# Low part of the first layer's weights summed on TensorE and written by ScalarE; the exponential of a block's weights one pair behind its subtraction

## The chip, the cores and the metric

The kernel runs on one core of one Trainium2 chip. Its time is the device time of one execution in microseconds; less is better. Three runs of the kernel before gave a median of 1271.37 us (1271.09 to 1273.05). One more execution was profiled; all durations below come from it.

## The reference

A dynamic convolution of 7 taps, whose weights are a softmax over the taps, is followed by two feed-forward layers, one with ELU and one with a hard swish. The weights w_in and w_out reach the kernel as 64-bit numbers, the activations in 32 bits.

```python
w = np.exp(wg - wg.max(-1)); w = w / (w.sum(-1) + 1e-9)      # (2, 4096, 8 heads, 7 taps)
x = einsum("bshk,bskhg->bshg", w, windows of x)               # 8192 tokens x 192
h = x @ w_in1                                                 # 192 x 2048
g = np.where(h > 0, h, np.exp(np.minimum(h, 0)) - 1)
x = g @ w_out1                                                # 2048 x 192
h = x @ w_in2
out = (h * np.clip(h + 3, 0, 6) / 6) @ w_out2
```

## The kernel before

**Blocks and pairs.** The 8192 tokens are cut into 16 blocks of 512. For each of the two layers (m) and each block (i) there are 8 *pairs* (q): a pair is two tiles of 128 of the 2048 hidden features. The list `cells` holds all 256 (m, i, q), and the main loop (L562) goes through them one by one; n is the number of the pair. In step n TensorE gets the first product of pair n (192 inputs to 2 x 128 features, into the PSUM banks `hset`) interleaved with the second product of pair n - 3 (2 x 128 features to 192 outputs, into the banks `acca` and `accb`). Both halves of TensorE's rows work side by side, so two matmuls of 64 rows and 512 columns run at once.

**High and low parts.** All products are made from a high and a low part (fp32r) of both factors: high by high, high by low, low by high. `round_g` (L440) writes the high part gh of the activations on ScalarE, `rest_g` (L444) the residual gl on VectorE.

**What follows a pair.** For both halves (k = 1, then 0): `act_a` (L428) makes relu and exp on ScalarE, `gate` (L448) ELU on VectorE. After the first half come `fold_b`, then `round_g` and `rest_g` of pair n - 1, then `fold_a`. `fold_b` (L301) is called three pairs after the last of a block: ScalarE copies accb into `fold` (L308). accb is one bank: the first second product of the next block waits for that copy. acca is two banks that alternate.

**Weights of layer one.** They are split in *units*: 8 of w_in (kind "i") and 8 of w_out ("o"), each 128 x 384. Group 0 is one unit, groups 1 to 7 two each, group 8 one. A unit passes `begin` (absolute value on ScalarE into a bank, `aux` or `acca[1]`), s0 to s2 (clamp, shift, sign: the high 32 bits of a double made into an fp32 number f), s3 (exponent on VectorE into `tr`, and ScalarE's copy of f as the high part), s4 (the double's low 32 bits scaled), s5 (f minus the high part) and s6 (plus the scaled low bits, written as the low part). s0 to s6 but for the copy are VectorE's. Groups 0 and 1 go ahead of the main loop, 2 and 3 in step 0, then one group per step up to step 5. Layer two's units go through the same steps, one per block of layer one, a few steps at a time (`Stream`, L488).

**The softmax and the convolution.** `attention` (L192) returns its work as a list: s0 (maximum and subtraction on VectorE, exponential on ScalarE), s1 (sum and reciprocal), s2 (product with it), then 14 operations on GpSimd that make the block's convolution. s0, s1, s2 of a later block are called in three successive steps, in the end of step n; from the third block on s0 falls on the step before that of `fold_b`. `prepare` (L274) transposes the block's result on TensorE, and ScalarE and VectorE (`xh`, `xl`) split it. For block 1 this is done in step 2, into the banks acca[0] and accb.

**Order.** The schedule is manual: every engine works in the order in which the program issues its instructions. DMAs stand on SP's queue; after the first steps they are kept in a list and issued at marks in TensorE's work (`transfers`).

Of the kernel before, what the change touches and what calls it, by code (L numbers as in the profile page):

```python
# [17 lines left out]
def kernel(  # L18
# [53 lines left out]
    accb, aux = psp.tile([P, 512], F32, name="accb"), psp.tile([P, 512], F32, name="aux")  # L72

    ident = cpool.tile([P, P], F32, name="ident")
    warm = cpool.tile([P, 1], F32, name="warm")


# [31 lines left out]
    class Unit:  # L109
# [19 lines left out]
        def begin(self):  # L129

            bank = acca[1] if self.m == 0 and self.kind == "o" else aux
            self.b = bank[:, 0:UN].bitcast(U32)
            nc.scalar.activation(self.b.bitcast(F32), self.hw.bitcast(F32), AF.Abs)

        def s0(self):
# [6 lines left out]

        def s2(self):
            nc.vector.scalar_tensor_tensor(
                self.b, self.hw, 0xC0000000, self.b, op0=ALU.bitwise_and, op1=ALU.bitwise_or)

        def s3(self):
            self.r = stage.tile([P, UN], U32, tag="tr", name="tr", bufs=2)
            nc.vector.tensor_scalar(self.r, self.b, 0xFF800000, None, op0=ALU.bitwise_and)
            hi, _, v = self.parts()  # L150
            nc.scalar.copy(hi, v(self.b.bitcast(F32)))  # L151

        def s4(self):
            f = self.r.bitcast(F32)
            nc.vector.scalar_tensor_tensor(f, self.lw, 2.0**-52, f, op0=ALU.mult, op1=ALU.mult)  # L155

        def s5(self):
            f, (hi, _, v) = self.b.bitcast(F32), self.parts()
# [33 lines left out]
    def attention(i):  # L192

        n = TM * H
        xt, w3 = blk.pop(i)
        shp = [P, n, K]
        tt = {}
        v = nc.vector
        hn = n // 2
        yt = xw.tile([P, 2 * N], F32, tag="y", name="y", bufs=YB)  # L200
        y, yd = yt[:, 0:XN].rearrange("p (t e) -> p t e", e=D), yt[:, XN:].rearrange("p (s c) -> p s c", s=2)
        ya[i] = y, yd
        tmp = xw.tile([P, TM, D], F32, tag="tmp", name="tmp")

        def s0():
            mx = tt["m"] = xw.tile([P, n, 1], F32, tag="mx", name="mx")
            v.tensor_reduce(mx, w3, axis=AX.X, op=ALU.max)
            v.tensor_tensor(w3, w3, mx.to_broadcast(shp), op=ALU.subtract)  # L208
            nc.scalar.activation(w3, w3, AF.Exp)

        def s1():
            s = tt["m"]
            v.tensor_reduce(s, w3, axis=AX.X, op=ALU.add)
            v.tensor_scalar_add(s, s, 1e-9)
            v.reciprocal(s, s)

        if i == 0:

            pw = hset[1][0][:, 0:hn * K].rearrange("p (a k) -> p a k", k=K)
            po = hset[0][0][:, 0:2 * D].rearrange("p (t e) -> p t e", e=D)  # L220
            hs = [(nc.vector, slice(0, 2), pw, po), (nc.gpsimd, slice(2, 4), w3[:, hn:, :], tmp[:, 0:2])]
        else:
            hs = [(nc.gpsimd, slice(0, TM), w3, tmp)]

        def s2():
            s = tt["m"]
            if i == 0:
                v.tensor_tensor(pw, w3[:, :hn, :], s[:, :hn, :].to_broadcast([P, hn, K]), op=ALU.mult)
                v.tensor_tensor(w3[:, hn:, :], w3[:, hn:, :], s[:, hn:, :].to_broadcast([P, hn, K]), op=ALU.mult)
            else:  # L230
                v.tensor_tensor(w3, w3, s.to_broadcast(shp), op=ALU.mult)

        def product(k):
            def s():
                for eng, t, w, o in hs:
                    nt = t.stop - t.start
                    xk = xt[:, t.start + k:t.stop + k, :].rearrange("p t (h g) -> p t h g", g=G)
                    wk = w[:, :, k:k + 1].to_broadcast([P, nt * H, G])
                    if k == K - 1:
                        o = y[:, t, :]  # L240
                    eng.tensor_tensor(  # L241
                        o.rearrange("p t (h g) -> p t h g", g=G), xk,
                        wk.rearrange("p (t h) g -> p t h g", h=H), op=ALU.mult)
            return s

        def add():
            for eng, t, _, o in hs:
                eng.tensor_tensor(y[:, t, :], y[:, t, :], o, op=ALU.add)

        def add_a():  # L250
            for eng, t, _, o in hs:
# [12 lines left out]

        steps = [s0, s1, s2, product(K - 1)]
        for k in range(K - 2, -1, -1):
            steps += [product(k)] + ([add] if k else [add_a, add_d])
        return steps
# [5 lines left out]
    def prepare(m, i):  # L274
# [2 lines left out]
        v = lambda t: t[:, 0].rearrange("p (h c) -> p h c", h=2)  # L277
        if m == 0:

            (y, yd), ps = ya.pop(i), hset[0] if i == 0 else (acca[0], accb) if i == 1 else (acca[i % 2], aux)  # L280
            for t in range(TM):
                for h, p in enumerate(half):
                    nc.tensor.transpose(ps[h][:, t * HP:(t + 1) * HP], y[p, t, 0:P], ident[p, p])  # L283
            for s in range(2):
                for h, p in enumerate(half):
                    nc.tensor.transpose(ps[h][:, HN + s * HP:HN + (s + 1) * HP], yd[p, s], ident[p, p])
            parts = [(ps[h][:, 0:XN // 2], (lambda h: lambda t: v(t)[:, h])(h)) for h in range(2)]
        else:
            parts = [(zin.pop(i)[:, 0:XN], lambda t: t[:, 0])]

        def split():
            for src, w in parts:
                nc.scalar.copy(w(X["h"]), src)
            for src, w in parts:
                nc.vector.tensor_tensor(w(X["l"]), src, w(X["h"]).bitcast(F32), op=ALU.subtract)
            for k in "hl":
                for a in range(2):
                    later(2, X[k][half[1 - a], 1].bitcast(F32), X[k][half[a], 0].bitcast(F32))
        return split

    def fold_b(m, i):  # L301
# [161 lines left out]
    first = {b: NQ * k for k, b in enumerate(order)}  # L463
    last = {b: NQ * k + NQ - 1 for k, b in enumerate(order)}
    prep = {b: max(0, first[b] - PREP) for b in order}
    prep[0, 1] = LAG - 1
    start2 = first[1, 0]
    ya, xts, rs, gg, blk, zs, zin, folds = {}, {}, {}, {}, {}, {}, {}, {}
    told = {}
# [43 lines left out]
    for n in range(2 * NQ):  # L513
        c = NQ * (n + 2) if n < NB - 2 else start2 + (NQ if n % 2 else 0)
        groups.append([("io"[n % 2], 1, n // 2)])
        wtasks.append([c - 3, c + (3 if n < NB - 2 else 2 if n % 2 else 6), 1])
    made = {}

    def want(n):
        if n < len(groups) and n not in made:  # L520
            made[n] = [Unit(*u) for u in groups[n]]

    def w_steps(n):
        def step(k, u):
            def s():
                if k < 0:
                    if u == 0:
                        want(n)
                        want(n + 1)
                    made[n][u].begin()  # L530
                else:
                    getattr(made[n][u], f"s{k}")()
            return s
        return [step(k, u) for k in range(-1, WS) for u in range(len(groups[n]))]

    wtasks = [
        [b, d, (WS + 1) * c, (lambda n: lambda: w_steps(n))(n)] for n, (b, d, c) in enumerate(wtasks) if n > 1]
    begin = {i: max(6, prep[0, i - 1]) for i in range(2, NB)}
    loads = {begin[i] - 5: i for i in begin}
    softmax = {}  # L540

    three = cpool.tile([P, 1], F32, name="three")
    with tc.manual_schedule():
        nc.vector.memset(three, 3.0)
        nc.scalar.activation(warm, three, AF.Exp)
        blk[0] = load_block(0, lambda: want(0))
        make_identity(nc, ident)
        blk[1] = load_block(1)

        todo = {"w": w_steps(0), "a": attention(0)}  # L550
        for k in "aaawwawawawawawaw":
            todo[k].pop(0)()
        for s in todo["a"] + todo["w"]:
            s()
        c1 = attention(1)
        for s in c1[:3]:
            s()
        prepare(0, 0)()
        for s in c1[3:] + w_steps(1):
            s()  # L560
        wst = Stream(wtasks)
        for n in range(len(cells) + LAG + 3):  # L562
            now = n
            jobs = []
            for m, i in order:
# [4 lines left out]
                if m and n == last[m, i] + LAG + 2 + (i < NB - 1):  # L570
                    jobs.append(give(i))
            matmuls(n)

            for k in (1, 0):
                if n < len(cells):
                    act_a(n, k)
                    gate(n, k)
                if not k:
                    continue
                for b in order:  # L580
                    if n == last[b] + LAG:
                        fold_b(*b)
                if 1 <= n <= len(cells):
                    round_g(n - 1)
                    rest_g(n - 1)
                for b in order:
                    if n == last[b] + LAG + 1:
                        fold_a(*b)
# [3 lines left out]
                f()  # L592
            for i in range(2, NB):

                k = n - (begin[i] - 3)
                if k == 0:
                    softmax[i] = attention(i)
                if 0 <= k < 3:
                    softmax[i].pop(0)()
                if k == 3:  # L600
                    for s in softmax.pop(i):
                        s()
            wst.run(n)
# [34 lines left out]
```

## Time and profile before

| | |
|---|---|
| median of 3 runs | 1271.37 us |
| profiled execution | 1270.2 us, its span 1268.4 us |
| TensorE busy | 1182.7 us, 93% |
| VectorE busy | 909.9 us, 72% |
| ScalarE busy | 849.8 us, 67% |
| GpSimd busy | 426.7 us, 34% |
| mean granted TensorE clock | 0.98 of full speed |

A busy share is a mean over stages with different limits: the first 100 us, in which weights are split, and the stretch behind them, in which TensorE seldom stands still, are read apart. Where an engine idles, the row says in brackets for how long and what ended it. On VectorE and ScalarE an instruction's listed duration is somewhat longer than the distance to the start of the next one; sums of a busy chain go from start to start.

### The profile page before, as it was taken

The page shows a single profiled execution, that of the slowest core. Times are in us where ns is not written, and L with a number is a line of the kernel's source. Part 1 is how long each engine was busy: PE and PEld are TensorE (multiplying, and loading weights), DVE is VectorE, ACT ScalarE, POOL GpSimd, SP SyncE. Part 2 cuts the span into 40 slices and gives each one's busy share as a digit, 9 for nine tenths or more (in the row PEclk, how much of TensorE's full clock was granted, in tenths as well). Part 3 has the DMA queues.
Part 4 walks back from the last instruction along what each step waited for, and adds up shares of the span by engine and source line. Part 5 has one row for each costly group of instructions (what it writes and reads, how often), then busy time and mean ns, then how long its engine had stood idle before and what let it go on. Part 6 is the DMA issues. An engine that isn't in the chain of part 4 may idle for free.

```text
span 1268.4 us, 25353 instructions
## 1 busy us (share of the span) xinstructions
PE 1182.7 (93%) x10112; PEld 1091.5 (86%) x10112; DVE 909.9 (72%) x1264; ACT 849.8 (67%) x1314; POOL 426.7 (34%) x234
## 2 busy tenths in 40 slices
PE   2379999999999999999999999999999999999998
PEld 1257898888888888888888899999999999999996
DVE  7998777877777877788777666666666666666663
ACT  2447778877787877787886556666665566666553
POOL 7408886666886666876300000000000000000000
PEclk9589999999999999999999999999999999999999
DMA  6421222112221212222111111111111111111110
GB/s 158 132 75 36 86 86 71 53 61 73 86 86 51 69 64 73 86 66 70 32 46 52 50 51 38 51 50 28 38 51 51 51 39 50 51 38 33 45 39 26
DMA packets 33686, 75.82 MB, mean 60 GB/s; under 512 B 4644, under 2 KB 17058, under 8 KB 33568
## 3 DMA queue, kind: packets, MB, share of 16 engines
q1 hardware_dynamic: 33568, 74.19, 20.4%
q8 instruction: 80, 1.31, 0.5%
q14 instruction: 38, 0.31, 0.1%
HBM read 36.43 MB, written 12.58 MB: 39 GB/s over the span
## 4 chain that ended last, share of the span: by engine, by line
PE 55%; DVE 1%; ACT 1%; issue 0%; DVEq 0%
PE h L415 25%; PE acca L415 17%; PE accb L415 12%; DVE gl L446 1%; DVE r L452 0%; PE acca L339 0%; PE aux L339 0%; ACT r L435 0%; ACT r L436 0%; ACT gh L442 0%; DVE tr L155 0%; DVE wt L208 0%; ACT fold L308 0%; PE acca L283 0%; DVE z L315 0%
## 5 line engine op out<-in xcount | busy, mean ns | idle before, releaser
L415 PE MATMUL h<-xh,wi_l 64*128 64x512 f32 x1536 | 566.5, 399 | 3.9 <-DVE wi_l L165 3.9
L415 PE MATMUL h<-xh,wi_h 64*128 64x512 f32 x1536 | 558.7, 398 | 7.4 <-ACT wi_h L151 2.8
L415 PE MATMUL acca<-gh,wo 64*128 64x512 f32 x2048 | 564.8, 395 | 0.3
L415 PE MATMUL h<-xl,wi_h 64*128 64x512 f32 x1536 | 555.6, 397 | 0.8 <-DMA xl<-xl 0.8
L446 DVE TENSOR_TENSOR gl<-r,gh 128x1024 fp32r<-128x1024 f32 x256 | 346.1, 1352 | 76.1 <-ACT gh L442 75.1
L415 PEld LDWEIGHTS acca<-gh,wo 64*128 64x128 f32 x2048 | 380.5, 186 | 18.5 <-SPq L419 2.4
L415 PE MATMUL accb<-gh,wo 64*128 64x512 f32 x1024 | 327.5, 399 | 45.0 <-ACT fold L308 22.7
L438 ACT ACTIVATE r<-h,three 128x512 f32<-128x512 f32 x256 | 176.5, 689 | 223.5 <-PE h L415 214.5
L415 PE MATMUL accb<-gl,wo 64*128 64x512 f32 x1024 | 323.1, 395 | 0.4 <-DVE gl L446 0.4
L415 PE MATMUL acca<-gl,wo 64*128 64x512 f32 x1024 | 321.3, 393 | 0.0
L415 PEld LDWEIGHTS h<-xh,wi_h 64*128 64x128 f32 x1536 | 277.7, 187 | 20.0 <-ACT wi_h L151 3.2
L415 PEld LDWEIGHTS h<-xh,wi_l 64*128 64x128 f32 x1536 | 278.2, 187 | 16.2 <-DVE wi_l L165 5.0
L455 DVE SCALAR_TENSOR_TENSOR r<-r,h 128x512 f32<-128x512 f32 x256 | 175.8, 687 | 161.6 <-ACT r L438 160.7
L415 PEld LDWEIGHTS h<-xl,wi_h 64*128 64x128 f32 x1536 | 277.8, 187 | 12.7 <-DMA xl<-xl 1.5
L442 ACT CAST gh<-r 128x1024 fp32r<-128x1024 f32 x256 | 266.2, 1040 | 3.7 <-DVE r L452 1.8
L452 DVE SCALAR_TENSOR_TENSOR r<-r,h 128x512 f32<-128x512 f32 x256 | 174.8, 683 | 93.4 <-ACT r L436 92.5
L415 PEld LDWEIGHTS accb<-gh,wo 64*128 64x128 f32 x1024 | 187.6, 187 | 58.0 <-ACT fold L308 28.5
L241 POOL TENSOR_TENSOR tmp<-xt,wt 128x768 f32<-128x768 f32 (+1 forms) x96 | 196.0, 2042 | 7.3 <-DMA xt<-in_x_dram 1.1
L415 PEld LDWEIGHTS accb<-gl,wo 64*128 64x128 f32 x1024 | 190.6, 186 | 8.0 <-DVE gl L446 0.8
L415 PEld LDWEIGHTS acca<-gl,wo 64*128 64x128 f32 x1024 | 190.2, 186 | 7.9
L435 ACT ACTIVATE r<-h 128x512 f32<-128x512 f32 x256 | 152.8, 597 | 54.4 <-PE acca L415 35.9
L436 ACT ACTIVATE r<-r 128x512 f32<-128x512 f32 x256 | 161.9, 633 | 8.3
(87 smaller groups left out, 704.4 us busy)
## 6 DMA issues: line engine op xcount, KB each, us to landing
xt<-in_x_dram SPq DMA_DIRECT2D x14, 960.0 KB, 4.8
xh<-xh SPq DMA_DIRECT2D x64, 192.0 KB, 2.7
xl<-xl SPq DMA_DIRECT2D x64, 192.0 KB, 2.9
raw<-in_moe_w_out_dram SPq DMA_DIRECT2D x16, 384.0 KB, 3.3
z<-z SPq DMA_DIRECT2D x16, 384.0 KB, 2.3
zin<-z SPq DMA_DIRECT2D x16, 384.0 KB, 3.0
out_dram<-ot SPq DMA_DIRECT2D x16, 384.0 KB, 3.9
raw<-in_moe_w_in_dram SPq DMA_DIRECT2D x16, 192.0 KB, 3.3
```

The lines of the kernel that those rows point to most:

```text
L241: eng.tensor_tensor(o.rearrange("p t (h g) -> p t h g", g=G), xk, wk.rearrange("p (t h) g -> p t h g", h=H), op=ALU.mult)
L415: mm = nc.tensor.matmul(o, w, r, start=st, stop=sp).ins
L435: nc.scalar.activation(r, h, AF.Relu, scale=-1.0)
L436: nc.scalar.activation(r, r, AF.Exp, scale=-1.0)
L438: nc.scalar.activation(r, h, AF.Relu, bias=three)
L442: nc.scalar.copy(gg[n][0], rs[n])
L446: nc.vector.tensor_tensor(gl, rs.pop(n), gh.bitcast(F32), op=ALU.subtract)
L452: nc.vector.scalar_tensor_tensor(r, r, -1.0, h, op0=ALU.add, op1=ALU.max)
L455: nc.vector.scalar_tensor_tensor(r, r, 6.0, h, op0=ALU.min, op1=ALU.mult)
```

## The change

**Weights of layer one.** s5 and s6 are gone for layer one. Instead f is written to a buffer in SBUF, s4 writes its result as fp32r (`rr`), and TensorE sums f times the identity, the high part times the negative identity and rr times the identity into the unit's bank (p5, after the matmuls of a step); ScalarE copies the sum out as the low part (p6, behind relu and exp of both halves). For groups 4 to 8 the absolute value is written into the SBUF buffer as well, and s0 to s3 work there. In the steps below 8 `round_g` and `rest_g` come after p6.

**Softmax.** The exponential is a step of its own, s0e, one pair behind the subtraction; the list starts two steps earlier and the load of its block three steps earlier. The convolution keeps its step.

**Also moved.** From step 8 on `round_g` and `rest_g` come ahead of `fold_b`. `prepare` of block 1 goes from step 2 to step 5 and uses hset[0] in place of acca[0] and accb.

```diff
+            if self.m == 0:
+                self.ps = bank[:, 0:UN]
+                self.f = fts[self.n][:, self.u * UN:(self.u + 1) * UN].bitcast(U32)
+                if self.n > 3:
+                    self.b = self.f
+            else:
+                self.f = self.b
             nc.scalar.activation(self.b.bitcast(F32), self.hw.bitcast(F32), AF.Abs)
...
+        def p5(self):
+
+            hi, _, v = self.parts()
+            nc.tensor.matmul(self.ps, ident, self.f.bitcast(F32), start=True, stop=False)
+            nc.tensor.matmul(v(self.ps), minus, hi, start=False, stop=False)
+            nc.tensor.matmul(self.ps, plus, self.rr, start=False, stop=True)
+
+        def p6(self):
+            _, los, v = self.parts()
+            for lo, c in los:
+                nc.scalar.copy(lo, v(self.ps)[..., c])
...
             v.tensor_tensor(w3, w3, mx.to_broadcast(shp), op=ALU.subtract)
+
+        def s0e():
             nc.scalar.activation(w3, w3, AF.Exp)
...
-            (y, yd), ps = ya.pop(i), hset[0] if i == 0 else (acca[0], accb) if i == 1 else (acca[i % 2], aux)
+            (y, yd), ps = ya.pop(i), hset[0] if i < 2 else (acca[i % 2], aux)
...
-    prep[0, 1] = LAG - 1
+    prep[0, 1] = 5
...
-    loads = {begin[i] - 5: i for i in begin}
+    loads = {max(0, begin[i] - 8): i for i in begin}
...
             matmuls(n)
+            if n < NQ:
+                for u in made[n + 1]:
+                    u.p5()
 
             for k in (1, 0):
                 if n < len(cells):
                     act_a(n, k)
                     gate(n, k)
+                if not k and n < NQ:
+                    for u in made[n + 1]:
+                        u.p6()
+                if k == (n >= NQ) and 1 <= n <= len(cells):
+                    round_g(n - 1)
+                    rest_g(n - 1)
                 if not k:
                     continue
                 for b in order:
                     if n == last[b] + LAG:
                         fold_b(*b)
-                if 1 <= n <= len(cells):
-                    round_g(n - 1)
-                    rest_g(n - 1)
...
-                k = n - (begin[i] - 3)
+                k = n - (begin[i] - 5)
```

Three places show what the edits do to the order. First ScalarE at a block boundary of layer one, before; L435 and L436 are relu and exp of a half, L209 the exponential of the softmax, L308 the fold, L442 gh.

```order
L442 CAST gh<-r 128x1024
L435 ACTIVATE r<-h_74 128x512
L436 ACTIVATE r<-r 128x512
L209 ACTIVATE wt<-wt 128x224
L435 ACTIVATE r<-h_73 128x512
L436 ACTIVATE r<-r 128x512
L308 COPY fold<-accb 128x512
L442 CAST gh<-r 128x1024
```

The same place with the change (L459, L460 are relu and exp, L332 is the fold, L466 gh):

```order
L459 ACTIVATE r<-h_74 128x512
L460 ACTIVATE r<-r 128x512
L459 ACTIVATE r<-h_73 128x512
L460 ACTIVATE r<-r 128x512
L466 CAST gh<-r 128x1024
L332 COPY fold<-accb 128x512
```

The exponential no longer stands between the relu and exp of the two pairs, and gh has moved from behind the fold to ahead of it.

Second, VectorE some two pairs earlier, with the change; L476 are gates, L470 is gl, L229 and L230 are the maximum and the subtraction, L157 is s3 of a unit of layer two.

```order
L476 SCALAR_TENSOR_TENSOR r<-r,h_75 128x512
L470 TENSOR_TENSOR gl<-r,gh 128x1024
L476 SCALAR_TENSOR_TENSOR r<-r,h_74 128x512
L229 TENSOR_REDUCE mx<-wt 128x32
L230 TENSOR_TENSOR wt<-wt,mx 128x224
L157 TENSOR_SCALAR tr<-aux 128x384
L476 SCALAR_TENSOR_TENSOR r<-r,h_73 128x512
L470 TENSOR_TENSOR gl<-r,gh 128x1024
```

Maximum and subtraction (L229, L230) have come to stand between the gate and s3; before, nothing stood there, and the two followed two pairs later:

```order
L452 SCALAR_TENSOR_TENSOR r<-r,h_74 128x512
L149 TENSOR_SCALAR tr<-aux 128x384
L452 SCALAR_TENSOR_TENSOR r<-r,h_73 128x512
L446 TENSOR_TENSOR gl<-r,gh 128x1024
L452 SCALAR_TENSOR_TENSOR r<-r,h_72 128x512
L155 SCALAR_TENSOR_TENSOR tr<-raw,tr 128x384
L452 SCALAR_TENSOR_TENSOR r<-r,h_75 128x512
L446 TENSOR_TENSOR gl<-r,gh 128x1024
L452 SCALAR_TENSOR_TENSOR r<-r,h_74 128x512
L207 TENSOR_REDUCE mx<-wt 128x32
L208 TENSOR_TENSOR wt<-wt,mx 128x224
```

Maximum and subtraction (L207, L208 there) stood directly behind the gate of the pair in which the fold comes; they have moved two pairs forward, ahead of an s3.

Third, ScalarE in one step of layer one's weights (step 2) with the change; L459 and L460 are relu and exp, L177 the low parts, L141 the absolute values of the next group, L159 its high parts.

```order
L459 ACTIVATE r<-h_73 128x512
L460 ACTIVATE r<-r 128x512
L459 ACTIVATE r<-h_72 128x512
L460 ACTIVATE r<-r 128x512
L177 CAST wi_l<-aux 128x384
L177 CAST wo_88<-acca_77 128x2x128
L177 CAST wo_88<-acca_77 128x2x64
L466 CAST gh<-r 128x1024
L233 ACTIVATE wt<-wt 128x224
L141 ACTIVATE f<-raw 128x384 x2
L159 CAST wi_h<-f 128x384
L159 CAST wo_88<-f 128x2x192
```

The low parts stand behind relu and exp of both halves and ahead of gh, and gh ahead of the next group's absolute values.

## Rows read from the trace of the kernel before

**Rows 1.** Busy by stretches: us, PE, PEld, DVE, ACT, POOL busy, TensorE's granted clock, DMA:

```profile
60.00:70.00 10.00, 7.77 (x44) 6.17 (x46) 9.27 (x20) 4.14 (x9) 0.00 (x0) 0.59 0.17 48
90.00:100.00 10.00, 7.33 (x37) 5.05 (x39) 9.83 (x17) 6.27 (x12) 6.63 (x4) 0.78 0.00 0
```

**Rows 2.** The waits of the whole span: who waited for whom, us, times, longest:

```profile
ACT wt L209 <- DVE wt L208: 45.8, 15, 7.6
...
PE accb L415 <- ACT fold L308: 22.7, 13, 2.4
```

**Rows 3.** Timeline of TensorE, a block boundary of layer two: start, us, work:

```profile
757.33 0.40 PE L415 MATMUL accb<-gh,wo 64*128 64x512 f32 x1
...
761.76 0.39 PE L415 MATMUL accb<-gh,wo 64*128 64x512 f32 x1
```

**Rows 4.** Timeline of TensorE, a block boundary of layer one:

```profile
225.10 0.40 PE L415 MATMUL accb<-gh,wo 64*128 64x512 f32 x1
...
231.41 0.49 PE L415 MATMUL accb<-gh,wo 64*128 64x512 f32 x1 [1.67 <-ACT fold L308]
```

**Rows 5.** Timeline of ScalarE, the same boundary:

```profile
218.89 0.48 ACT L151 CAST wi_h<-aux 128x384 fp32r<-128x384 f32 x1 [1.22 <-DVE tr L149]
...
229.35 0.39 ACT L209 ACTIVATE wt<-wt 128x224 f32<-128x224 f32 x1 [2.78 <-DVE wt L208]
...
230.79 0.57 ACT L308 COPY fold<-accb 128x512 f32<-128x512 f32 x1
```

**Rows 6.** Timeline of VectorE, the same boundary:

```profile
218.30 0.55 DVE L149 TENSOR_SCALAR tr<-aux 128x384 uint32<-128x384 uint32 x1
...
227.83 0.67 DVE L452 SCALAR_TENSOR_TENSOR r<-r,h 128x512 f32<-128x512 f32 x1
228.43 0.37 DVE L207 TENSOR_REDUCE mx<-wt 128x32 f32<-128x224 f32 x1
228.91 0.41 DVE L208 TENSOR_TENSOR wt<-wt,mx 128x224 f32<-128x224 f32 x1
```

**Rows 7.** Timeline of ScalarE, one step of the weights of layer one:

```profile
55.62 0.48 ACT L151 CAST wi_h<-aux 128x384 fp32r<-128x384 f32 x1 [4.77 <-DVE tr L149]
...
56.46 0.60 ACT L435 ACTIVATE r<-h 128x512 f32<-128x512 f32 x1
...
57.63 1.03 ACT L442 CAST gh<-r 128x1024 fp32r<-128x1024 f32 x1
...
58.57 0.59 ACT L435 ACTIVATE r<-h 128x512 f32<-128x512 f32 x1
```

**Rows 8.** Timeline of ScalarE, the boundary of layer two:

```profile
760.09 0.59 ACT L308 COPY fold<-accb 128x512 f32<-128x512 f32 x1 [0.17 <-PE accb L415]
```

**Rows 9.** The page, costliest groups: POOL's products of a block, mean ns behind the comma:

```profile
L241 POOL TENSOR_TENSOR tmp<-xt,wt 128x768 f32<-128x768 f32 (+1 forms) x96 | 196.0, 2042 | 7.3 <-DMA xt<-in_x_dram 1.1
```

**Rows 10.** Timeline of VectorE, the weights of layer one:

```profile
52.26 0.55 DVE L137 TENSOR_SCALAR aux<-aux 128x384 f32<-128x384 f32 x1
...
57.84 0.54 DVE L165 TENSOR_TENSOR wi_l<-aux,tr 128x384 fp32r<-128x384 f32 x1
58.31 0.60 DVE L165 TENSOR_TENSOR wo<-acca,tr 128x256 fp32r<-128x256 f32 x2
...
59.43 1.21 DVE L446 TENSOR_TENSOR gl<-r,gh 128x1024 fp32r<-128x1024 f32 x1
60.57 0.67 DVE L452 SCALAR_TENSOR_TENSOR r<-r,h 128x512 f32<-128x512 f32 x1
...
83.73 0.54 DVE L137 TENSOR_SCALAR aux<-aux 128x384 f32<-128x384 f32 x1
```

**Rows 11.** Timeline of TensorE, the same stage and the first boundary:

```profile
62.23 0.79 PE L415 MATMUL accb<-gh,wo 64*128 64x512 f32 x1 [14.03 <-DVE xl L295]
...
100.39 0.62 PE L415 MATMUL accb<-gh,wo 64*128 64x512 f32 x1
...
116.52 0.50 PE L415 MATMUL accb<-gh,wo 64*128 64x512 f32 x1 [1.05 <-ACT fold L308]
```

More of the change, by code (lines that the diff above doesn't have):

```diff
@@ L74 @@
     ident = cpool.tile([P, P], F32, name="ident")
+    plus, minus = (cpool.tile([P, P], F32R, name=n) for n in ("plus", "minus"))
     warm = cpool.tile([P, 1], F32, name="warm")
@@ L144, in s2 @@
             nc.vector.scalar_tensor_tensor(
-                self.b, self.hw, 0xC0000000, self.b, op0=ALU.bitwise_and, op1=ALU.bitwise_or)
+                self.f, self.hw, 0xC0000000, self.b, op0=ALU.bitwise_and, op1=ALU.bitwise_or)
         def s3(self):
             self.r = stage.tile([P, UN], U32, tag="tr", name="tr", bufs=2)
-            nc.vector.tensor_scalar(self.r, self.b, 0xFF800000, None, op0=ALU.bitwise_and)
+            nc.vector.tensor_scalar(self.r, self.f, 0xFF800000, None, op0=ALU.bitwise_and)
             hi, _, v = self.parts()
-            nc.scalar.copy(hi, v(self.b.bitcast(F32)))
+            nc.scalar.copy(hi, v(self.f.bitcast(F32)))
         def s4(self):
-            f = self.r.bitcast(F32)
-            nc.vector.scalar_tensor_tensor(f, self.lw, 2.0**-52, f, op0=ALU.mult, op1=ALU.mult)
+            f = o = self.r.bitcast(F32)
+            if self.m == 0:
+                o = self.rr = stage.tile([P, UN], F32R, tag="rr", name="rr", bufs=2)
+            nc.vector.scalar_tensor_tensor(o, self.lw, 2.0**-52, f, op0=ALU.mult, op1=ALU.mult)
+        def p5(self):
[7 more added lines that the diff above has]
+                nc.scalar.copy(lo, v(self.ps)[..., c])
         def s5(self):
@@ L262, in add_d @@
                     eng.tensor_tensor(yd.rearrange("p s (a e) -> p s a e", a=2), v(y), v(o), op=ALU.add)
-        steps = [s0, s1, s2, product(K - 1)]
+        steps = [s0, s0e, s1, s2, product(K - 1)]
         for k in range(K - 2, -1, -1):
@@ L297, in split @@
                 for a in range(2):
-                    later(2, X[k][half[1 - a], 1].bitcast(F32), X[k][half[a], 0].bitcast(F32))
+                    later(1 if (m, i) == (0, 1) else 2, X[k][half[1 - a], 1].bitcast(F32), X[k][half[a], 0].bitcast(F32))
         return split
@@ L516 @@
         wtasks.append([c - 3, c + (3 if n < NB - 2 else 2 if n % 2 else 6), 1])
-    made = {}
+    made, fts = {}, {}
     def want(n):
@@ L521, in want @@
             made[n] = [Unit(*u) for u in groups[n]]
+            for u, unit in enumerate(made[n]):
+                unit.n, unit.u = n, u
     def w_steps(n):
@@ L529, in s @@
                         want(n + 1)
+                        if groups[n][0][1] == 0:
+                            fts[n] = act.tile([P, XN], F32, tag="z", name="f", bufs=2)
                     made[n][u].begin()
@@ L533, in step @@
             return s
-        return [step(k, u) for k in range(-1, WS) for u in range(len(groups[n]))]
+        return [step(k, u) for k in range(-1, WS if groups[n][0][1] else 5) for u in range(len(groups[n]))]
     wtasks = [
-        [b, d, (WS + 1) * c, (lambda n: lambda: w_steps(n))(n)] for n, (b, d, c) in enumerate(wtasks) if n > 1]
+        [b, d, ((WS if groups[n][0][1] else 5) + 1) * c, (lambda n: lambda: w_steps(n))(n)] for n, (b, d, c) in enumerate(wtasks) if n > 1]
     begin = {i: max(6, prep[0, i - 1]) for i in range(2, NB)}
-    loads = {begin[i] - 5: i for i in begin}
+    loads = {max(0, begin[i] - 8): i for i in begin}
     softmax = {}
@@ L547 @@
         make_identity(nc, ident)
+        nc.scalar.copy(plus, ident)
+        nc.scalar.mul(minus, ident, -1.0)
         blk[1] = load_block(1)
         todo = {"w": w_steps(0), "a": attention(0)}
-        for k in "aaawwawawawawawaw":
+        for k in "aaaawwawawawaw":
             todo[k].pop(0)()
@@ L554 @@
             s()
+        made[0][0].p5()
+        made[0][0].p6()
         c1 = attention(1)
-        for s in c1[:3]:
+        for s in c1[:4]:
             s()
         prepare(0, 0)()
-        for s in c1[3:] + w_steps(1):
+        for s in c1[4:] + w_steps(1):
             s()
@@ L593 @@
             for i in range(2, NB):
-                k = n - (begin[i] - 3)
+                k = n - (begin[i] - 5)
                 if k == 0:
                     softmax[i] = attention(i)
-                if 0 <= k < 3:
+                if 0 <= k < 4:
                     softmax[i].pop(0)()
-                if k == 3:
+                if k == 5:
                     for s in softmax.pop(i):
```

## Prediction

> **What bounds the kernel now.** I read four views in this order: busy time by stretches, the waits, the timelines of the engines round one block boundary, and the timelines of the stage in which the first layer's weights are split.
>
> The stretches [rows 1] show two regimes. Between 60 and 100 us VectorE is busy 9.27 and 9.83 of 10 us, while TensorE has gaps and a granted clock of 0.59 and 0.78 of full speed: here VectorE's chain sets the pace. Behind that TensorE is the bound, and what counts is only the time in which it stands still.
>
> The waits [rows 2] name that time: TensorE waits 22.7 us, 13 times, for ScalarE's `fold` copy, which empties the bank accb at a boundary between two blocks. ScalarE itself waits 45.8 us, 15 times, for the softmax subtraction before its exponential.
>
> One boundary shows the link. A pair of TensorE takes 4.43 us (757.33 to 761.76 on the undisturbed boundary of layer two [rows 3]), so after 225.10 the next pair is due at 229.53; it starts at 231.41, 1.88 us late, and 1.67 of this are listed as idle [rows 4]. ScalarE sat 2.78 us before the exponential at 229.35, then did relu, exp and the fold at 230.79, which took 0.57 [rows 5]. VectorE was late with the subtraction (228.91), because the gate of the half before ran at 227.83 and the maximum at 228.43 [rows 6]. VectorE in turn was late through an earlier link: the copy of layer-two weights at 218.89 waited 1.22 us for VectorE's `tr` at 218.30, and relu, exp, gate and the next residual queue behind it.
>
> **The exponential a pair behind its subtraction.** The subtraction moves two pairs earlier, the exponential one, so ScalarE finds its operand ready: the 2.78 us go. What is late next? Two things are moved into this chain. First, maximum and subtraction (0.48 from start to start, then 0.41 long, some 0.8 together [rows 6]) now stand directly ahead of `tr`, so `tr`, the copy behind it, relu, exp and all gates up to the one at 227.83 come 0.8 us later: that gate runs 228.63 to 229.30. Second, `gh` of the pair before stands ahead of the fold now, and it needs this very gate. So gh starts at 229.35, takes 0.94 (57.63 to 58.57 [rows 7]), the fold runs 230.29 to 230.86, and TensorE starts at 230.91 instead of 231.41. Gain 0.5 us of 1.88 per boundary; 13 boundaries have an exponential in them, 6.5 us. The ends: the wait gone altogether gives 13 x 1.67 = 21.7 us; if VectorE's delay costs a full gh more, (0.94 - 0.5) x 13 = 5.7 us are lost. I take 6.5, since every link of it has a row.
>
> In layer two the fold also goes behind gh, at 16 boundaries. There ScalarE was early: the fold waited 0.17 us for accb [rows 8]. gh would start at 759.9, take 0.94, the fold end at 761.4; the bank is wanted at 761.76 [rows 3]. 0.35 us of cover are left, cost nothing; if gh came late by more than that, each further tenth costs 1.6 us over the 16.
>
> The loads of a block (two DMAs on SP's queue) go out three pairs earlier. Their buffers belong to the block two before, whose 14 GpSimd operations take 14 x 2.04 = 28.6 us [rows 9], 6.4 pairs, from a start 8 pairs ahead of the new load: 1.6 pairs of cover, some 7 us. Cost nothing.
>
> **The weights of layer one.** Each of 16 units loses the subtraction (0.47, from start to start, 57.84 to 58.31 [rows 10]) and the sum (0.47, or about 0.53 for the pair of the w_out units): 16 x 0.47 + 8 x 0.47 + 8 x 0.53 = 15.5 us of VectorE. If VectorE stayed the bound, the whole of it were won. It does not, because what replaces it is a ring through three engines. In one step: VectorE's first five operations on a pair of units, 5 x 0.47 = 2.35; ScalarE's two copies of the high part, 0.84; relu and exp of two halves, 2 x 1.17; the three new copies of the low part, 1.0 (the same columns as the 0.84, one instruction more); gh 0.94; VectorE's residual gl 1.14; hand-offs 0.2. Sum 8.8 us [rows 7, 10], and no link can overlap the next, since ScalarE works in program order: the low copies stand ahead of gh, gh ahead of gl, gl ahead of the next pair of units. TensorE's six new matmuls per step lie beside relu and exp: at the rate of the 512-column matmuls (0.23 at full, 0.43 at half clock) they are 1.1 to 1.9 us, under 2.34. The bank must be empty before the next Abs or the next sum: this adds waits only in the first steps.
>
> For true FP32 the Trainium skill (FP8 and Floating Point Precision, TensorE Precision Notes) says four passes; no matmul of this form is in the trace. By it, the identity product of each unit is four times as long, the six together about 1.9 at full and 3.8 at half clock, which at half clock would lengthen a ring by 1.5.
>
> The step of before is (83.73 - 52.26) / 3 = 10.5 us [rows 10]. Up to 52.26 seven units have been through, 6.8 us less work; against that come max and subtraction (0.8), waits for the emptied bank, and gh behind the low copies ahead of the first gl. I take a lead of 2 there (ends 0 and 6.8). Three rings and 1.3 us of softmax work make 27.7 instead of 31.5: lead 5.8.
>
> Now TensorE. The transposes of block 1 move from the third pair to the sixth and into the bank pair that the seventh pair (cell 6) wants, so cell 6 waits until VectorE's `xl` has read it, one ring and 0.9 us behind 83.73 - 5.8: 87.6. TensorE has then stood some 6 us. After the 14.03 us gap at 62.23 [rows 11] the clock of the next 10 us was 0.59 [rows 1], that is the lower level for more than half of it. I charge 2.8 us: cell 6 lasts until 94.8, relu, exp and low copies bring cell 7 to 97, cell 8 to 102.5. Before, cell 8 started at 100.39 [rows 11]. From there to the first boundary before took 16.13 us (116.52), now 3 x 4.43 and 0.6 of waiting, 13.9: 2.2 won back. So at 116.5 both kernels stand level. One price here is an upper bound: 0.47 is from operations whose operand lies in a PSUM bank, while Abs's result of groups 4 to 8 now lies in SBUF, and the trace has no such one-source operation of 384 columns. Its ends are 0.47 and a saving of almost all of it, 4 x 0.4 per ring in five rings, 8 us. I take 0.42, near the row: 1 us. The other end is 10 us lost, if TensorE ran at half clock in these cells and became the long link of the ring.
>
> Sum against the profiled execution, 1270.2 us (span 1268.4 and 1.8 around it): -6.5 - 1 = 1262.7. The median of the runs is 1271.4, 1.2 above it: 1264.
>
> **Rivals.** *The SBUF operations are twice as fast.* Streaming 384 columns at half the time saves 0.2 on each of the four on the ring, 0.8 in five rings, 4 us in place of 1: 1261. This is the Trainium skill's rule (VectorE: DVE Perf Modes, Mode 2x_2P: one source and the destination in SBUF); no operation in the trace shows it. Against it stands only that no row bears it out; for it that the bank was left for SBUF in five groups.
>
> *The fold's wait goes altogether.* If gh is ready early because the 0.8 us on VectorE vanish in its pauses, 21.7 - 1 in place of 6.5: 1264 - 15 = 1249. For it: in layer two, with no exponential, TensorE has no such wait. Against: the gate at 227.83 and the maximum behind it show no idle time ahead of them [rows 6]; there is no pause there to take the 0.8 up.
>
> *Nothing is won at the boundary*, since gh takes what the exponential gave back: 1270.
>
> *Slower.* The fold behind gh makes TensorE wait where it did not: in layer two, 16 times. It decides from 0.35 us of lateness on; one gh late by a whole 0.94 costs 0.6 x 16 = 9.5 us, less 7: 1274. For it: the cover is thin; against: ScalarE idles a microsecond ahead of each half there, so nothing makes gh late. The same time comes out if the setup runs at half clock (10 lost): 1274.
>
> **Numbers.** Forecast 0.36 (own range 1260 to 1268), twice as fast in SBUF 0.27, wait gone 0.12, nothing at the boundary 0.12, slower 0.13. What a measurement tells from no change is 0.2%, 2.5 us: faster than 1268.9 is 0.75 of it, within 0.13, slower 0.12. The range for eight in ten goes from half of the full gain, 1251, to just under the slower case, 1273.
>
> **What would show it.** Right: the 13 waits of accb for fold stand at about 1.2 us instead of 1.67, with gh directly ahead of the fold and a gate ahead of gh; no wait of the exponential for the subtraction; rings of 8 to 9 us in the setup, with VectorE idle before each gl; TensorE idle some 5 us ahead of cell 6. Wrong: boundaries without a wait; a setup in which VectorE is still busy throughout; new waits of accb in layer two; TensorE at the lower clock between 45 and 85 us.

## The result, and the profile after

The median went from 1271.69 us to 1255.23 us (4 runs each), a ratio of 0.9869 (95% interval 0.9852 to 0.9886): 16.5 us faster. The forecast was 1264, 7.4 us faster. The profiled execution took 1254.9 us, its span 1253.1, 15.3 less than before.

Where these microseconds went is read from one instruction that every block has, the fold on ScalarE. The distance from the start of one fold to the start of the next is the period of a block; the first fold closes the setup, the stage in which the weights of layer one are split.

| | before | after |
|---|---|---|
| first fold | 115.89 | 117.28 |
| period of a block, layer one (mean of the six distances between the folds of blocks 2 to 8) | 38.26 | 37.14 |
| first to 16th fold | 569.4 | 554.8 |
| period of a block, layer two | 35.84 | 35.84 |

So the setup lost 1.4 us and layer one won 14.6. The rest of the 15.3 is 1.5 at the change of layers, where two folds are 37.5 to 39.0 us apart even in kernels that are alike there, which is not explained here, and 0.6 at the end. There the last two folds are 33.1 to 33.2 us apart in the three kernels of this document that have gh ahead of the fold, and 33.8 in the others, so the 0.6 goes with that move.

The waits answer to [rows 2]: that of accb for the fold is 6.9 us in place of 22.7, and what is new is a wait of 5.0 us in the setup. ScalarE's exponential waits 4.8 us once, in place of 45.8 in 15 waits.

```profile
PE h L439 <- DVE xl L319: 7.6, 2, 5.0
...
PE accb L439 <- ACT fold L332: 6.9, 12, 0.6
...
ACT wt L233 <- DVE wt L230: 4.8, 1, 4.8
```

The boundary that answers to [rows 4 to 6], first TensorE, then ScalarE, then VectorE (start, us, work):

```profile
224.13 0.40 PE L439 MATMUL accb<-gh,wo 64*128 64x512 f32 x1
...
229.35 0.50 PE L439 MATMUL accb<-gh,wo 64*128 64x512 f32 x1 [0.57 <-ACT fold L332]
```

```profile
219.46 0.48 ACT L159 CAST wi_h<-aux 128x384 fp32r<-128x384 f32 x1 [2.77 <-DVE tr L157]
...
227.78 1.03 ACT L466 CAST gh<-r 128x1024 fp32r<-128x1024 f32 x1
228.72 0.58 ACT L332 COPY fold<-accb 128x512 f32<-128x512 f32 x1
```

```profile
215.06 2.24 DVE L470 TENSOR_TENSOR gl<-r,gh 128x1024 fp32r<-128x1024 f32 x1
...
218.30 0.65 DVE L230 TENSOR_TENSOR wt<-wt,mx 128x224 f32<-128x224 f32 x1
218.88 0.55 DVE L157 TENSOR_SCALAR tr<-aux 128x384 uint32<-128x384 uint32 x1
...
222.07 1.29 DVE L470 TENSOR_TENSOR gl<-r,gh 128x1024 fp32r<-128x1024 f32 x1 [0.25 <-ACT gh L466]
...
223.89 1.05 DVE L165 SCALAR_TENSOR_TENSOR tr<-raw,tr 128x384 f32<-128x384 uint32 x1
...
225.60 1.23 DVE L470 TENSOR_TENSOR gl<-r,gh 128x1024 fp32r<-128x1024 f32 x1
226.76 0.69 DVE L476 SCALAR_TENSOR_TENSOR r<-r,h 128x512 f32<-128x512 f32 x1
```

ScalarE waits 2.77 us for `tr`, and from 219.46 to the fold at 228.72 no row of it shows a pause. `gh` at 227.78, directly ahead of the fold, waits for nothing: its gate, 0.69 us from 226.76, ended 0.33 us earlier.

To set the two kernels side by side, count from the start of TensorE's pair ahead of the boundary: 225.10 before [rows 4], 224.13 after. From there the gate begins 2.63 us later; before, it was 2.73 [rows 6]. The forecast put it at 3.53 (228.63) and let it hold gh up.

Why was VectorE early? Its rows of before in the same stretch, to be set beside the two `gl` and the s4 above (1.29 at 222.07, 1.05 at 223.89, 1.23 at 225.60):

```profile
200.59 0.39 DVE L231 TENSOR_TENSOR wt<-wt,mx 128x224 f32<-128x224 f32 x1
...
221.51 1.78 DVE L446 TENSOR_TENSOR gl<-r,gh 128x1024 fp32r<-128x1024 f32 x1 [0.25 <-ACT gh L442]
...
223.81 1.61 DVE L155 SCALAR_TENSOR_TENSOR tr<-raw,tr 128x384 f32<-128x384 uint32 x1
...
225.94 1.97 DVE L446 TENSOR_TENSOR gl<-r,gh 128x1024 fp32r<-128x1024 f32 x1
```

Their 1.78, 1.61 and 1.97 us are not what these operations cost: alone, gl takes 1.23, and the second operation of s4 takes 0.55 (short convolution, below). Beside them GpSimd was at work on the convolution, until 229.91; after, it ends at 225.55. On the same count `tr` begins 1.55 us later than before (5.25 ahead of the pair in place of 6.80), not 0.8, as the gl ahead of it takes 2.24 beside GpSimd (215.06); the three operations, 1.79 us shorter together, give that back. First and last operation of GpSimd, before and after:

```profile
201.19 1.55 POOL L241 TENSOR_TENSOR y<-xt,wt 128x768 f32<-128x768 f32 x1 [9.53 <-PE accb L415]
...
229.02 0.89 POOL L262 TENSOR_TENSOR y<-y,tmp 128x256 f32<-128x256 f32 x1
```

```profile
197.71 1.64 POOL L265 TENSOR_TENSOR y<-xt,wt 128x768 f32<-128x768 f32 x1 [9.31 <-PE aux L310]
...
224.49 1.06 POOL L286 TENSOR_TENSOR y<-y,tmp 128x256 f32<-128x256 f32 x1
```

Before, the convolution began behind the product of the weights with the reciprocal (200.59 above). The change moves that product one pair forward with the list, so GpSimd now begins behind the transposes. Against the fold of its block it ends 3.2 us ahead in place of 0.9.

### The profile page after: what moved, and what is told of

It is laid out like the page before. It is cut to its first block, busy times and chain, and to the rows that moved or that the text cites. A ratio compares the mean times of both kernels' runs of the same rounds, so it can differ in the third digit from the quotient of the medians.

```text
span 1253.1 us, 25450 instructions
## 1 busy us (share of the span) xinstructions
PE 1200.7 (96%) x10176; PEld 1093.3 (87%) x10176; DVE 938.6 (75%) x1224; ACT 852.9 (68%) x1340; POOL 414.4 (33%) x234
## 4 chain that ended last, share of the span: by engine, by line
PE 68%; ACT 15%; DVE 12%; issue 3%; DMA 1%; SPq 0%; DVEq 0%; ACTq 0%
PE h L439 31%; PE acca L439 21%; PE accb L439 14%; DVE gl L470 5%; ACT gh L466 4%; ACT r L459 4%; ACT r L460 4%; DVE r L476 2%; DMA xl<-xl 1%; DVE tr L157 1%; DVE wt L230 1%; DVE aux L148 1%; DMA xt<-in_x_dram 1%; ACT fold L332 1%; ACT aux L141 0%
## 5 line engine op out<-in xcount | busy, mean ns | idle before, releaser
L470 DVE TENSOR_TENSOR gl<-r,gh 128x1024 fp32r<-128x1024 f32 x256 | 377.3, 1474 | 56.7 <-ACT gh L466 55.3
L439 PEld LDWEIGHTS h<-xh,wi_l 64*128 64x128 f32 x1536 | 279.0, 186 | 15.3 <-ACT wi_l L177 2.9
L466 ACT CAST gh<-r 128x1024 fp32r<-128x1024 f32 x256 | 265.8, 1038 | 1.4 <-DVE r L479 0.8
L476 DVE SCALAR_TENSOR_TENSOR r<-r,h 128x512 f32<-128x512 f32 x256 | 174.1, 682 | 52.0 <-ACT r L460 51.5
L459 ACT ACTIVATE r<-h 128x512 f32<-128x512 f32 x256 | 152.7, 596 | 61.9 <-PE acca L439 31.3
L460 ACT ACTIVATE r<-r 128x512 f32<-128x512 f32 x256 | 162.0, 633 | 8.1
```

Source lines behind the costliest of these rows:

```text
L439: mm = nc.tensor.matmul(o, w, r, start=st, stop=sp).ins
L459: nc.scalar.activation(r, h, AF.Relu, scale=-1.0)
L460: nc.scalar.activation(r, r, AF.Exp, scale=-1.0)
L466: nc.scalar.copy(gg[n][0], rs[n])
L470: nc.vector.tensor_tensor(gl, rs.pop(n), gh.bitcast(F32), op=ALU.subtract)
L476: nc.vector.scalar_tensor_tensor(r, r, -1.0, h, op0=ALU.add, op1=ALU.max)
```

## The experiments

Eleven kernels ran; each is compared with the kernel before by runs on the same chip. Periods and first folds are from the starts of the folds, as above. Every forecast of these runs names rival theories by letters; the text says which one the run bears out.

| run | median us | ratio to before (interval) | first fold | period |
|---|---|---|---|---|
| fold first | 1244.45 | 0.9783 (0.9768 to 0.9799) | 116.83 | 36.30 |
| product late | 1268.44 | 0.9970 (0.9958 to 0.9983) | 116.64 | 38.35 |
| gh first, on before | 1298.61 | 1.0218 (1.0197 to 1.0240) | 116.45 | 40.86 |
| softmax part only | 1242.80 | 0.9768 (0.9753 to 0.9782) | 113.72 | 36.28 |
| weights part only | 1269.74 | 0.9997 (0.9986 to 1.0009) | 119.25 | 38.26 |
| short convolution, on before | 1250.60 | 0.9848 (0.9832 to 0.9865) | 115.16 | 37.01 |
| bank, fold first | 1246.36 | 0.9811 (0.9794 to 0.9829) | 119.06 | 36.31 |
| early transposes, fold first | 1260.31 | 0.9921 (0.9906 to 0.9937) | 131.41 | 36.30 |
| product late, fold first | 1253.06 | 0.9852 (0.9837 to 0.9866) | 115.22 | 37.35 |
| exponential in the same pair | 1244.13 | 0.9786 (0.9770 to 0.9802) | 115.20 | 36.29 |
| softmax part, groups 4 to 6 in SBUF | 1240.24 | 0.9752 (0.9737 to 0.9766) | 111.39 | 36.29 |

**Fold first.** The changed kernel, with the fold ahead of gh again.

```diff
-                if k == (n >= NQ) and 1 <= n <= len(cells):
+                if k == 0 and 1 <= n < NQ:
                     round_g(n - 1); rest_g(n - 1)
...
                         fold_b(*b)
+                if NQ <= n <= len(cells):
+                    round_g(n - 1); rest_g(n - 1)
```

> The changed kernel with one move undone: from step 8 on the fold stands ahead of gh again. Theory A (the rest of the boundary wait is ScalarE's queue: after the change it works without a pause from the copy at 219.46 to the fold at 228.72, and gh in it is never kept waiting): the fold comes 0.94 us earlier, the wait of 0.57 us goes at all 12 boundaries, 6.9 us less, 1248.3. Theory B (VectorE's gates set the fold): the wait stays at 0.57, 1255 to 1256. Theory C (with the pause gone TensorE runs into the next late link, as gh and gl come half a microsecond later): no gain, or a wait at another place, 1252 to 1257.

Theory A, and more: 10.8 us in place of 6.9. The wait is gone from the list of waits, and the period falls by 0.84, where the wait showed 0.57. On ScalarE the copy and the fold of the same boundary are 8.32 us apart in place of 9.26, by one gh:

```profile
218.03 0.48 ACT L159 CAST wi_h<-aux 128x384 fp32r<-128x384 f32 x1 [2.77 <-DVE tr L157]
...
226.35 0.57 ACT L332 COPY fold<-accb 128x512 f32<-128x512 f32 x1
```

**Product late.** The changed kernel, but sum, reciprocal and product are not taken in a row; the product waits a pair, as before the change.

```diff
-                if 0 <= k < 4:
+                if 0 <= k < 3 or k == 4:
```

> The changed kernel, but the product of a block's weights with the reciprocal comes one pair later, where it stood before the change, so GpSimd starts the convolution some 2.4 us later in the block and ends it behind the boundary's gates again. Theory A (GpSimd and VectorE hold each other up, and the change gained at the boundary mainly by letting GpSimd finish earlier): the two last gl ahead of the fold take 1.8 to 2.0 us again in place of 1.29 and 1.23, the wait of accb for the fold grows from 0.57 to 1.2 us or more, 7 us or more slower, 1262 or more. Theory B (the exponential out of the way and the order on VectorE made the gain): within 1.5 us of the changed kernel, wait 0.5 to 0.7.

Theory A in its time: all but 3 of the 16.5 us are given back. The wait of accb for the fold is 1.2 us at most (0.6 in the changed kernel). The place is not quite the one expected. The last gl takes 1.72, but the larger part is the subtraction ahead of `tr`: 2.03 us in place of 0.65, with the copy on ScalarE behind it.

```profile
218.47 2.03 DVE L230 TENSOR_TENSOR wt<-wt,mx 128x224 f32<-128x224 f32 x1
...
227.24 1.72 DVE L470 TENSOR_TENSOR gl<-r,gh 128x1024 fp32r<-128x1024 f32 x1
```

```profile
220.99 0.48 ACT L159 CAST wi_h<-aux 128x384 fp32r<-128x384 f32 x1 [3.65 <-DVE tr L157]
...
230.54 0.58 ACT L332 COPY fold<-accb 128x512 f32<-128x512 f32 x1
```

**Product late, fold first.** Both edits together.

> Fourth corner of a square: the changed kernel with both the product of the weights one pair later (GpSimd late, as in the run with 38.35 us a block) and the fold ahead of gh (as in the run with 36.30). Theory A (the two costs add: GpSimd's phase 1.2 us a block, gh ahead of the fold 0.85): 37.5 us a block, about 1257. Theory B (with the fold first there is enough cover for GpSimd's phase to cost nothing): 36.3, 1244 to 1246.

Theory A: 37.35, so GpSimd's later start costs 1.05 us a block with the fold first and 1.21 with gh first; the two costs nearly add. No wait for the fold is left in this kernel's list, yet its period is 1 us above 36.30. Between two folds neither half of TensorE's rows works for 0.45 us only (0.06 with the fold first alone); the rest must lie where one half waits alone.

```profile
218.41 0.48 ACT L159 CAST wi_h<-aux 128x384 fp32r<-128x384 f32 x1 [3.68 <-DVE tr L157]
...
226.72 0.57 ACT L332 COPY fold<-accb 128x512 f32<-128x512 f32 x1
```

From the copy to the fold ScalarE takes 8.31 us, as with the fold first alone (8.32). But it waits 3.68 us for `tr` in place of 2.77, so 0.91 of the 1.05 enters there. How this reaches TensorE without a wait for the fold stays open.

**gh first, on before.**

```diff
+                if n >= NQ and n <= len(cells):
+                    round_g(n - 1); rest_g(n - 1)
                 for b in order:
                     if n == last[b] + LAG:
                         fold_b(*b)
-                if 1 <= n <= len(cells):
+                if 1 <= n < NQ:
```

> The kernel before with one move of the change alone: from step 8 on gh and gl stand ahead of the fold. Theory A (ScalarE's queue sets the fold): the fold comes 0.94 us later at 13 boundaries, the wait goes from 1.75 to about 2.6, 12 us slower, 1283; nothing in layer two, where 0.35 us of cover are left. Theory B (the move is part of the gain): same or faster, 1265 to 1272.

Theory A has the sign, but 27 us in place of 12. Two more things come with the longer wait, up to 3.5 us; what each of them is worth was not tested. GpSimd's work falls on other operations of VectorE (gl at 226.76 takes 2.65), and behind the wait TensorE's matmuls are slower: 0.62 us at 320.18 beside the usual 0.39, in a stretch whose granted clock is 0.83, so for a part at the lower of its two levels.

```profile
319.74 0.64 PE L415 MATMUL accb<-gh,wo 64*128 64x512 f32 x1 [3.48 <-ACT fold L308]
...
320.18 0.62 PE L415 MATMUL accb<-gh,wo 64*128 64x512 f32 x1
```

```profile
320.00:330.00 10.00, 10.00 (x82) 8.36 (x82) 6.63 (x13) 7.35 (x13) 0.95 (x1) 0.83 0.01 2
```

**Softmax part only**, on the kernel before: the hunks on s0e, `begin[i] - 5`, the steps and the loads.

> The kernel before with the softmax part of the change alone: maximum and subtraction two pairs earlier, exponential one, sum, reciprocal and product one, the loads three; the fold stays ahead of gh, the weights of layer one are split as before. Theory A (GpSimd finishes ahead of the boundary and ScalarE's queue has no gh ahead of the fold): no wait at the boundary, 1.75 x 13 = 22.7 us less, 1249. Theory B (my forecast: VectorE's gate comes 0.8 us later): wait of about 0.3 (1.2 without the gh), 1253 or more.

28.9 us faster, more than theory A's 22.7, as no wait for the fold is left. The first fold comes 2.2 us earlier too; the first boundary's own wait for the fold, 1.05 us before [rows 11], is a part of this. This half of the change alone beats the whole by 12 us.

**Weights part only**, with the fold ahead of gh:

> The kernel before with the weights part of the change alone (sums on TensorE, low parts by ScalarE, block 1's transposes in step 5); softmax as before, fold ahead of gh from step 8 on. Theory A (at the boundary this part changes nothing, in the setup its ring gains 2 us up to cell 4 and loses more than that at cell 6, where TensorE waits 5 us for xl and then runs at the lower clock): period of a block 38.25 as before, first fold 1 to 3 us later, 1272 to 1275. Theory B (the 15.5 us taken from VectorE are worth something): 1262 to 1268.

No difference that can be told. The boundary is that of before, and the first fold comes 3.4 us later, a little more than theory A's 1 to 3; the median is below its range.

**Exponential in the same pair** as its subtraction, on the softmax part:

```diff
-                if 0 <= k < 4:
+                for _ in range({0: 2, 2: 1, 3: 1}.get(k, 0)):
```

> The kernel before with the softmax part of the change alone (1242.80), but with the exponential in the same pair as its subtraction, two pairs earlier than before the change. Theory A (what the softmax part won came from GpSimd's earlier start and from the place of the pause: ScalarE waits 2.77 us for tr there in any case): 36.3 us a block, within 2 us of 1242.80. Theory B (the exponential's distance from its subtraction is what counts): the exponential waits for its subtraction again and the fold comes late: 36.9 us a block or more, 1250 or more.

Theory A. ScalarE waits for the subtraction again, but in the place where it waited for `tr`:

```profile
215.30 0.39 ACT L211 ACTIVATE wt<-wt 128x224 f32<-128x224 f32 x1 [2.31 <-DVE wt L208]
215.77 0.48 ACT L151 CAST wi_h<-aux 128x384 fp32r<-128x384 f32 x1
...
223.82 0.57 ACT L310 COPY fold<-accb 128x512 f32<-128x512 f32 x1
```

By these rows it is not the distance between subtraction and exponential that counts, but that both left the dense stretch ahead of the fold.

**Short convolution, on before.**

```diff
-        for k in range(K - 2, -1, -1):
+        for k in range(0 if i > 1 else K - 2, -1, -1):
```

> The kernel before, with the convolution of blocks 2 to 15 cut from 7 taps to 2 (GpSimd does 4 operations a block in place of 14; the five middle taps are left out). Nothing else moves. Theory A (GpSimd's operations lengthen VectorE's two-operand ones): gl takes 1.23 us throughout in place of up to 1.97, the gates before the boundary come 1.2 us or more earlier, the wait for the fold falls from 1.75 to 0.5 or less, the period of a block from 38.25 to 37.0 or less, 16 to 22 us less: 1249 to 1256. Theory B (VectorE's durations have another cause, and the exponential's place in the order makes the wait): 1268 to 1273.

Theory A. With the old order and the exponential still waiting, 20 us go; gl takes 1.23 and the second operation of s4 0.55 in place of 1.61:

```profile
218.12 1.23 DVE L446 TENSOR_TENSOR gl<-r,gh 128x1024 fp32r<-128x1024 f32 x1 [0.25 <-ACT gh L442]
...
219.89 0.55 DVE L155 SCALAR_TENSOR_TENSOR tr<-raw,tr 128x384 f32<-128x384 uint32 x1
...
221.39 1.23 DVE L446 TENSOR_TENSOR gl<-r,gh 128x1024 fp32r<-128x1024 f32 x1 [0.25 <-ACT gh L442]
```

```profile
224.73 0.39 ACT L209 ACTIVATE wt<-wt 128x224 f32<-128x224 f32 x1 [1.54 <-DVE wt L208]
...
226.18 0.57 ACT L308 COPY fold<-accb 128x512 f32<-128x512 f32 x1
```

**Bank, fold first**: the two lines on `self.n > 3` are taken out.

> The changed kernel with the fold ahead of gh from step 8 on (as in the run that did this alone, 1244.45), and with the absolute values of groups 4 to 8 written into the PSUM bank, as for groups 0 to 3, and not into SBUF. Theory A (one-source operations within SBUF take half the time): clamp and shift take 0.47 from start to start in place of 0.27, each ring of the setup is 0.8 us longer, cell 4's gl 1.5 to 2.5 us later; given back at the single unit of group 8, whose clamp and shift took 1.03 and 1.59 beside GpSimd's operations and take 0.47 in a bank: 1243 to 1247. Theory B (the bank makes no difference): gl of cell 4 at the same time to 0.3 us.

Theory A at the rows: a clamp takes 0.47 from start to start in the bank; in SBUF, with the change, two of them take 0.54, 0.27 each.

```profile
54.62 0.56 DVE L143 TENSOR_SCALAR aux<-aux 128x384 f32<-128x384 f32 x1
55.09 0.56 DVE L143 TENSOR_SCALAR acca<-acca 128x384 f32<-128x384 f32 x1
```

```profile
54.91 0.62 DVE L145 TENSOR_SCALAR f<-f 128x384 f32<-128x384 f32 x2
55.45 0.62 DVE L148 TENSOR_SCALAR f<-f 128x384 uint32<-128x384 uint32 x2
```

Cell 4's gl comes at 89.26 in place of 86.25 (fold first), a little later than expected, and the first fold 2.2 us later. The two intervals overlap, so the times do not show this loss.

**Early transposes, fold first**: `prep[0, 1] = LAG - 1` and the old banks.

> The changed kernel with the fold ahead of gh from step 8 on, and with the transposes of block 1 back in step 2, in the banks acca[0] and accb. Theory A (their new place made cell 6 wait 5.0 us for xl and run at the lower clock behind that, while in step 2 TensorE waits for the weights anyway): no wait of 5 us ahead of cell 6, a wait of accb for xl at cell 3's second product that costs less, the first fold 2 to 6 us earlier, 1239 to 1243. Theory B (xl takes its time from the ring wherever it stands): within 1.5 us of 1244.45.

Both theories fail: 15.9 us slower than with the fold first alone. accb's wait for xl, 6.7 us, delays the identity products of that step behind it, and with it every later ring by some 5 us. The last ring with two units then falls into GpSimd's convolution. On SBUF two shifts take 3.33 us, where they take 0.62:

```profile
85.27 3.33 DVE L148 TENSOR_SCALAR f<-f 128x384 uint32<-128x384 uint32 x2
88.52 4.00 DVE L152 SCALAR_TENSOR_TENSOR f<-raw,f 128x384 uint32<-128x384 uint32 x2
```

```profile
85.04 1.72 POOL L265 TENSOR_TENSOR y<-xt,wt 128x768 f32<-128x768 f32 x1 [38.50 <-PE accb L439]
```

The changed kernel has this too, for the single unit behind cell 6: shift 1.59, s2 2.07.

```profile
90.05 1.59 DVE L148 TENSOR_SCALAR f<-f 128x384 uint32<-128x384 uint32 x1
91.67 2.07 DVE L152 SCALAR_TENSOR_TENSOR f<-raw,f 128x384 uint32<-128x384 uint32 x1
```

**Softmax part, groups 4 to 6 in SBUF.** VectorE still forms the low parts.

```diff
+            if self.m == 0 and 4 <= self.n <= 6:
+                self.b = fts[self.n][:, self.u * UN:(self.u + 1) * UN].bitcast(U32)
```

> A version meant to beat both kernels: the kernel before with the softmax part alone (1242.80), and the units of groups 4 to 6 worked in SBUF in place of the PSUM bank; VectorE still forms the low parts. Theory A (clamp, shift and exponent within SBUF take 0.27 in place of 0.47 while GpSimd is idle, and VectorE sets the pace there): 3 x 2 x 3 x 0.2 = 3.6 us less, 1238 to 1241. Theory B (GpSimd starts in this stretch and holds these operations up): 1243 or more.

The best of all: 1240.24, 15 us under the changed kernel. Its first fold comes 2.3 us before that of the softmax part alone; the two intervals overlap, so this last step is shown by the trace and not by the times.

## Why the prediction was off

- **What bounds.** Right: the fold's wait in layer one and VectorE's chain in the setup were the two places. But the 15.5 us taken off that chain were worth nothing that can be told (weights part only: 0.9997).
- **The exponential.** Its term of 6.5 us is the one that failed: layer one won 14.6, and the wait for the fold stood at 0.57 us, 12 times, in place of about 1.2, 13 times. The step that failed is the delay of the gate: "tr, the copy behind it, relu, exp and all gates up to the one at 227.83 come 0.8 us later". It carried VectorE's durations over from before, 1.78, 1.61 and 1.97, as if they belonged to the operations. They belonged to GpSimd's work beside them, which the change moves: the gate came 0.10 us earlier in its pair in place of 0.8 later, and 1.12 us a block were won in place of 0.5. Four periods part the effect of the order from that of GpSimd: 38.26 before; 37.01 without most of GpSimd's work in the old order; 37.35 in the new order with GpSimd late; 36.30 in the new order with GpSimd early.
- **The diff's list.** The forecast counted the loads and the subtraction that move with the list, but not that the product with the reciprocal moves too, and that the convolution, whose step stands still, waits for it.
- **gh ahead of the fold.** Its price of 0.94 was in the sum, and measured at 0.84 a block (1.00 with the product late). But it was taken to be kept waiting by its gate, which the rows do not show. That it would be the whole of what the fold still costs was not seen.
- **The rival in which the wait goes altogether** was given 0.12, with the argument that VectorE had no pause to take 0.8 us up. It needed none: three of its operations became 1.79 us shorter. With gh behind the fold it is what happened.
- **Layer two.** Right: no new wait, period 35.84 as before. The loads cost nothing, as forecast.
- **The setup.** Level was forecast with 1 us to the good; it lost 1.4. The term that failed is the lead of 2 us at 52.26 [rows 10], the first clamp of group 4: with the change it starts at 54.91, a lag of 2.65. The lead counted operations that go. But f now lies in SBUF, and beside GpSimd, which works on block 1's convolution until 46.49, the two exponents of group 1 take 3.28 us from start to start in place of 0.93, and the two of s4 3.91 in place of 2.76; in group 2 it is 1.89 for 0.94 and 3.89 for 2.55. Group 3 then waits 1.38 and 1.36 us for the identity products, with TensorE's granted clock at 0.50, its lower level. Group 1 before, then after:

```profile
27.22 0.55 DVE L149 TENSOR_SCALAR tr<-aux 128x384 uint32<-128x384 uint32 x1
...
28.15 2.84 DVE L155 SCALAR_TENSOR_TENSOR tr<-raw,tr 128x384 f32<-128x384 uint32 x2
```

```profile
26.43 3.36 DVE L157 TENSOR_SCALAR tr<-f 128x384 uint32<-128x384 uint32 x2
29.71 3.99 DVE L165 SCALAR_TENSOR_TENSOR rr<-raw,tr 128x384 fp32r<-128x384 uint32 x2
```

The rings behind that were faster than the forecast: 7.9, 8.8 (with 0.9 of softmax work) and 8.1 us from start to start of the clamps (54.91, 62.79, 71.57, 79.69), 24.8 in place of 27.7. The rival of twice as fast SBUF operations was right in its mechanism, and its 0.8 per ring is in those numbers. The Trainium skill's rule (VectorE: DVE Perf Modes, Mode 2×_2P) agrees with the rows, 0.27 for 0.47. Cell 6's wait was 5.0 for "some 6", with the lower clock behind it (0.84 and 0.81 are the means of two stretches). GpSimd lengthens the last unit's operations too (1.59 and 2.07 above); what this costs is not parted, since the run that spares them it, in the bank, has slower rings as well.

```profile
89.11 0.79 PE L439 MATMUL h<-xh,wi_h 64*128 64x512 f32 x1 [5.00 <-DVE xl L319]
```

```profile
80.00:90.00 10.00, 5.00 (x34) 3.33 (x32) 8.30 (x16) 6.19 (x13) 5.84 (x4) 0.84 0.21 68
90.00:100.00 10.00, 10.00 (x61) 7.32 (x61) 7.38 (x8) 4.85 (x9) 9.61 (x6) 0.81 0.25 66
```

## What to carry to other kernels

A duration in a trace belongs to an operation and to what runs beside it. Before carrying a VectorE row over to a new order, compare it with the same operation where GpSimd is idle, and when an edit moves work, ask which waiting engine is thereby released earlier. Where a copy frees a bank that the bound engine wants, nothing that can come later should stand ahead of it.

## What the runs showed of the hardware

Operations of VectorE with two sources in SBUF, and the one-source clamps, shifts and exponents from SBUF to SBUF, grew when GpSimd worked beside them, at most to about the length of a GpSimd operation: gl from 1.23 to as much as 2.68 us (before, at 101.25), the subtraction from 0.39 to 2.03, a shift from 0.27 to 1.6. With an operand in a PSUM bank they kept their time: gates 0.63 to 0.69 throughout layer one. So did the maximum, a reduction with its one source in SBUF: 0.37 to 0.38 with and without GpSimd. The Trainium skill (SBUF — State Buffer, SBUF: two separate sides) says that the two engines share a pair of ports, which one instruction holds to its end while the other waits; the rows agree. So for a clamp or a shift the place that is twice as fast alone (0.27 for 0.47) is the slower one beside GpSimd (1.6 for 0.47).
